# Attention with a two-level mixture of experts: units 30 to 41 of the script reordered, late rows of v loaded at their beginning, item 3 turned on TensorE

## The chip, the cores and the metric

The kernel runs on one core of one Trainium2 chip. The core has five engines that run side by side, each with its own program, in order: TensorE (PE in the profile; its weight loads are PEld), VectorE (DVE), ScalarE (ACT), GpSimd (POOL) and SyncE (SP). They wait for one another by semaphores. SyncE and GpSimd issue DMA transfers here; GpSimd's are indirect, by a list of row numbers. The metric is the device time of one execution in microseconds, as the median of several runs.

## The reference, cut to what matters

Channel attention over four batches: the columns of q and k are normed over the 3648 rows of a batch, a 256 x 256 score matrix is softmaxed, and v is multiplied by it. The result, 14592 rows of 256, goes through a mixture of experts: each row picks one of four groups and one of four experts in it (both by argmax), and each expert is two matrix products with a ReLU between.

```python
qn = q / (np.linalg.norm(q, axis=1, keepdims=True) + 1e-06)
kn = k / (np.linalg.norm(k, axis=1, keepdims=True) + 1e-06)
s = kn.transpose(0, 2, 1) @ qn / tau
...
attn = v @ a                                  # a = softmax(s); (4, 3648, 256)
x = attn.reshape(14592, 256)
g_idx = np.argmax(x @ w_group, axis=1)        # 4 groups
e_idx = np.argmax(xg @ w_expert[g], axis=1)   # 4 experts in each
h = np.maximum(xg[mask_e] @ w1[g, e], 0.0)    # 256 -> 1024
ye = h @ w2[g, e]                             # 1024 -> 256
out[tok_idx] = combined[:, None] * ye         # by the two softmax weights
```

## The kernel before

**Units.** A batch is cut into eight units: seven of 4 x 128 rows and one of 64 rows; four batches make 32 units. Each unit passes two stages. In the first its q and k are loaded and a score matrix is added up on TensorE (tile sacc, L210). After the eighth unit of a batch softmax(b) turns it into the matrix ahi, alo (the two parts of a split that keeps full precision with fast products), through the steps sm, se, ax, atp, awp and ahi. In the second stage a unit's rows of v are loaded (x_load, L278, tile vr), turned by eight TensorE transposes (x_tr, L290, tile vtr), split by ScalarE into vth (L291) and by VectorE into vtl (L292), and multiplied (x_mm, L309, tile xmm: for each of four blocks of 128 rows six matmuls). ScalarE copies each block into xs (L312); VectorE copies its 20 logits into L (L315). Turns of unit u+1 are issued ahead of the products of unit u.

**Routing.** routing(b, j0, j1) is a generator over 16 or 13 blocks of 128 rows, advanced by calls of advance(). It finds each row's expert (m, z, oh: L333 to L355), counts (inc L359, rs L363, two small matmuls pp on TensorE L365, bs L369), and gives each row a slot in a table sorted by expert (sf, si: L376, L378) and a weight (RECIPROCAL into xs, L391). Then GpSimd writes the rows to the table x_sorted, one indirect DMA for 128 rows (scatter, L411, some 1.5 us each on GpSimd with what stands between). After the first half of batch 2 has been routed, tables_pre (L504 to L462 in the lists) finds the first three items.

**Items.** An item is 512 rows of one expert; there are 28. The first three (KPRE) are taken from rows of the batches 0, 1 and the first half of 2 and read by plain DMA (fetch_x, L622); the others are gathered by GpSimd (L485, tile xg) once all rows are in the table. An item's rows are turned into xth, xtl, and each of its eight blocks has six matmuls hmm (ffn1, L827), a ReLU by ScalarE (hh, L831) and VectorE (hl, L832), and twelve matmuls yacc (ffn2, L843) two blocks later. The weights w1, w2 of an item are loaded into raw buffers by SyncE (fetch_w, L609) and split into halves by ScalarE (wh, L654) and VectorE (wl, L655). The first three items are turned by eight TensorE transposes (split_x, L689, tile xtr) with copies by ScalarE (L690) and VectorE (L691). Items from the fourth on (number 3) are turned by sixteen DMAs that re-block them (quads_of, L632, tile xq) and one VectorE STREAM_TRANSPOSE (turn_x, L676, tile xT).

**Order.** Up to unit 29 of the first stage a scheduler orders the engines. Then come script units t = 30 to 41 (TM = 30, k = t - TM = 0 to 11), in which the second stage's unit is x = t - 10 = 20 to 31; from there to the beginning of the items the program order written in the code is each engine's order. After that a scheduler has TensorE, ScalarE and VectorE until item 2, while SyncE and GpSimd stay in written order.

**Space.** v has three buffers (vp). q, k and their squares stand in a pool sp_ that is closed at k = 1. A ring of ten tiles (RING) is shared in turn by the xs of the units, the xg, xq and xT of the items and the results ys: a new tile waits until the one ten places back has been read. So xs of unit 31 takes the place of xs of unit 22, and xg of item 1 that of unit 21. There are three raw buffers for weights.

Of the kernel before, what the change touches and what calls it, by code (L numbers as in the profile page):

```python
# [52 lines left out]
XOFF = GPB + 2  # L53
TM = US - 2
# [3 lines left out]
def attention_moe(ctx: ExitStack, tc, q, k, v, tau, w_group, w_expert, w1, w2, out):  # L58
# [216 lines left out]
    def x_load(u):  # L275
        rows, nj = rows_of(u % GPB)
        vr = vp.tile([P, GJ, C], F32, tag="vr", name="vr", bufs=3)
        SP.dma_start(vr[:rows, :nj, :], tiles_of(v, u // GPB, u % GPB))  # L278
        xu[u] = dict(vr=vr)
# [15 lines left out]
    def x_mm(u, mid=None):  # L295
# [17 lines left out]
        if mid is not None:  # L313
            mid()
# [8 lines left out]
    def routing(b, j0=0, j1=NJ):  # L323
# [68 lines left out]
        pend.extend(((b, j0), now[0], j, si) for j in range(nj))  # L392

# [263 lines left out]
    def split_w(i, which, part=None):  # L657

        if not whs:
            for n in range(4):  # L660
                for l, nm in ((whs, "wh"), (wls, "wl")):
                    l.append(wp.tile([P, 2048], F32R, name=f"{nm}{n}", bufs=1) if n < 3 else None)
# [16 lines left out]
    def split_x(d):  # L679
# [18 lines left out]
        tokens(d["ids"], d["xg"][:, :, C], slot4, d["nv"], None if d is items[0] or "xT" in d else ins)  # L698
# [68 lines left out]
    soft = lambda n=1: [next(sgen, None) for _ in range(n)]  # L767
    for t in range(TM, len(xs_at)):
# [3 lines left out]
        if x + 2 < UX:  # L772
            x_load(x + 2)
        if k == 0:
            soft(2)
        if x + 1 < UX:
            x_tr(x + 1)
        if k == 0:
            s_mm(US - 2)
            s_mm(US - 1)  # L780
            advance(2)
            soft()
        if k == 1:
            sp_.close()
        if k == 2:
            soft(2)
        if k == 4:
            wp = ctx.enter_context(tc.tile_pool(name="wp", bufs=4))
            fetch_w(items[0], tb_pre, 0, "w1")
            fetch_w(items[0], tb_pre, 0, "w2")  # L790
        if x == UX - 3:
            fetch_x(items[0], tb_pre, 0)
        if x == UX - 1:
# [3 lines left out]
        def mid():  # L797
# [15 lines left out]
        if k > 8:  # L813
            advance(1)
        scatter(8)
        queue(x)
    vp_.close()
# [230 lines left out]
    for n in range(len(seq) + lag):  # L1048
        if n == 1:
            fetch_w(items[1], tb_pre, 1, "w1")  # L1050
# [7 lines left out]
        if n < len(seq):  # L1058
# [18 lines left out]
            if f == 7 and KPRE <= i + 2 < NBIG:  # L1077
# [45 lines left out]
        if n >= 1:  # L1123
            advance(20 if n >= 3 else 1)
# [87 lines left out]
```

## Time and profile before

| | us |
|---|---|
| three runs: lowest, median, highest | 1006.2, 1006.58, 1008.39 |
| profiled execution | 1007.67 |
| its span, first to last instruction | 1005.9 |

| engine | busy in the span, us | share |
|---|---|---|
| TensorE | 937.9 | 93% |
| VectorE | 610.2 | 61% |
| ScalarE | 469.7 | 47% |
| GpSimd | 351.9 | 35% |

How to read it: a row of a timeline has its start in us from the beginning of the span, its length, the engine, the line, the operation, the tiles written and read, and in brackets the time for which the engine stood idle just before, with what ended that. A row with "x8" is eight instructions of a kind in a row. "issue" means that the profile shows no other cause. PEclk is the share of TensorE's full clock. The first 30 script units take some 195 us of the span, the twelve in question end near 275 us, and the items fill the rest.

### The profile page before, as it was taken

What the parts mean: (1) busy time and instruction counts of PE and PEld (TensorE: products, weight loads), DVE (VectorE), ACT (ScalarE), POOL (GpSimd) and SP (SyncE); (2) the same over time, 40 slices, a digit from 0 to 9 for tenths busy, and PEclk for the clock granted to TensorE, in tenths of its full rate; (3) what the DMA queues carried; (4) which work ended last, traced back from release to release, by engine and by line L of the source; (5) the groups of instructions that cost most, each with busy time, mean ns of one, the idle gap of its engine ahead of it and who ended that gap; (6) DMA issues with size and microseconds to landing.
All of it is one profiled execution on the core that took longest, in us unless ns stands there. A gap on an engine that the chain in (4) does not pass through costs nothing.

```text
span 1005.9 us, 17880 instructions
## 1 busy us (share of the span) xinstructions
PE 937.9 (93%) x6228; PEld 820.5 (82%) x6228; DVE 610.2 (61%) x1140; ACT 469.7 (47%) x738; POOL 351.9 (35%) x426
## 2 busy tenths in 40 slices
PE   7998999886799569999999999999999999999994
PEld 6898989876688458888888888888888888888884
DVE  6888868655699355555555555555555645555541
ACT  6787567544553034444444444444444444444431
POOL 0005879854668613222222231222222222222111
PEclk9999999987899879999999999999999999999998
DMA  8947688336545345677777777777777677767730
GB/s 299 357 175 262 224 271 266 126 98 223 184 157 214 104 132 166 227 233 233 236 232 233 230 237 226 237 233 242 239 230 236 228 239 236 234 230 239 227 131 26
DMA packets 163188, 215.06 MB, mean 214 GB/s; under 512 B 67635, under 2 KB 121659, under 8 KB 163088
## 3 DMA queue, kind: packets, MB, share of 16 engines
q1 hardware_dynamic: 146512, 168.70, 52.9%
q0 software_dynamic: 15088, 45.10, 12.2%
q8 instruction: 51, 0.84, 0.4%
q14 instruction: 49, 0.40, 0.1%
q10 hardware_dynamic: 1488, 0.02, 0.1%
HBM read 170.33 MB, written 31.39 MB: 201 GB/s over the span
## 4 chain that ended last, share of the span: by engine, by line
PE 61%; issue 2%; SPq 1%; POOL 1%; DMA 0%; DVE 0%; ACT 0%; POOLq 0%; DVEq 0%; ACTq 0%
PE yacc L843 29%; PE hmm L827 27%; PE qacc L945 2%; PE qmm L928 2%; SPq L632 1%; PE qtr L935 1%; POOL out L853 0%; DMA out<-ys,ids 0%; DMA xq<-xg 0%; PE qxt L919 0%; DVE xT L676 0%; DVE hl L832 0%; POOL x_sorted L564 0%; DVE ys L852 0%; ACT wh L654 0%
## 5 line engine op out<-in xcount | busy, mean ns | idle before, releaser
L832 DVE SCALAR_TENSOR_TENSOR hl<-hmm,hh 128x512 fp32r<-128x512 f32 x224 | 153.8, 687 | 253.3 <-ACT hh L831 246.1
L831 ACT ACTIVATE hh<-hmm 128x512 fp32r<-128x512 f32 x224 | 132.6, 596 | 361.2 <-PE hmm L827 296.3
L853 POOL DMA_INDIRECT out<-ys,ids x112 | 127.7, 1140 | 461.5 <-ACT ys L850 434.1
L843 PE MATMUL yacc<-wh,hl 128*128 128x256 f32 x896 | 253.9, 283 | 17.6 <-DVE hl L832 16.5
L843 PE MATMUL yacc<-wh,hh 128*128 128x256 f32 x896 | 257.4, 287 | 4.5 <-DVE ys L852 4.5
L843 PE MATMUL yacc<-wl,hh 128*128 128x256 f32 x896 | 252.9, 282 | 0.0
L843 PEld LDWEIGHTS yacc<-wh,hh 128*128 128x128 f32 x896 | 169.9, 190 | 29.3 <-issue 12.2
L843 PEld LDWEIGHTS yacc<-wh,hl 128*128 128x128 f32 x896 | 170.4, 190 | 18.1 <-DVE hl L832 17.1
L827 PE MATMUL hmm<-xtl,wh 128*128 128x512 f32 x448 | 179.6, 401 | 3.2 <-DVE xtl L691 3.2
L827 PE MATMUL hmm<-xth,wh 128*128 128x512 f32 x448 | 179.6, 401 | 0.5 <-ACT xs L312 0.3
L827 PE MATMUL hmm<-xth,wl 128*128 128x512 f32 x448 | 177.9, 397 | 0.0
L843 PEld LDWEIGHTS yacc<-wl,hh 128*128 128x128 f32 x896 | 170.1, 190 | 7.9
L411 POOL DMA_INDIRECT x_sorted<-xs,si x116 | 142.4, 1228 | 84.9 <-issue 33.3
L655 DVE TENSOR_TENSOR wl<-wraw,wh 128x1024 fp32r<-128x1024 f32 x112 | 137.0, 1223 | 22.4 <-ACT wh L654 15.5
L654 ACT ACTIVATE wh<-wraw 128x1024 fp32r<-128x1024 f32 x112 | 117.8, 1053 | 4.4 <-DMA wraw<-in_moe_w 2.9
L827 PEld LDWEIGHTS hmm<-xth,wl 128*128 128x128 f32 x448 | 85.0, 190 | 20.5
L827 PEld LDWEIGHTS hmm<-xtl,wh 128*128 128x128 f32 x448 | 85.4, 191 | 14.1 <-DVE xtl L691 3.5
L827 PEld LDWEIGHTS hmm<-xth,wh 128*128 128x128 f32 x448 | 85.7, 191 | 12.4 <-ACT xs L312 1.0
L210 PE MATMUL sacc<-qkraw 128*128 128x256 f32 (+1 forms) x352 | 85.7, 389 | 6.5 <-DMA qkraw<-in_k 6.5
L210 PEld LDWEIGHTS sacc<-qkraw 128*128 128x128 f32 (+1 forms) x352 | 65.6, 195 | 15.4 <-DMA qkraw<-in_q 6.0
L309 PE MATMUL xmm<-ahi,vth 128*128 128x276 f32 (+1 forms) x232 | 71.6, 310 | 3.2 <-ACT xs L312 3.2
L309 PE MATMUL xmm<-alo,vth 128*128 128x276 f32 (+1 forms) x232 | 69.8, 301 | 0.0
(240 smaller groups left out, 1174.0 us busy)
## 6 DMA issues: line engine op xcount, KB each, us to landing
wraw<-in_moe_w SPq DMA_DIRECT2D x56, 1024.0 KB
wraw<-in_moe_w SPq DMA_DIRECT2D x96, 512.0 KB
vr<-in_v SPq DMA_DIRECT2D x28, 512.0 KB
qkraw<-in_q SPq DMA_DIRECT2D x27, 512.0 KB
qkraw<-in_k SPq DMA_DIRECT2D x27, 512.0 KB
xq<-xg SPq DMA_DIRECT2D x400, 32.0 KB
x_sorted<-xs,si POOLq DMA_INDIRECT x116
out<-ys,ids POOLq DMA_INDIRECT x112
```

The lines of the kernel that those rows point to most:

```text
L210: PE.matmul(d["acc"][:, c, :], kt[:rows, 1, cs], qt[:rows, 0, :], start=d.pop("first", True) and c == 0, stop=(g == NG), skip_group_check= ...
L309: PE.matmul(mm[:rows, :NE], vt[:, c, j * P:j * P + rows], at[:, c, :], start=(n == 0), stop=(n == 5))
L411: ins = POOL.indirect_dma_start(out=xs_d, out_offset=bass.IndirectOffsetOnAxis(ap=si[:rows, j:j + 1], axis=0), in_=xs[:rows, t, 0:RW].bitc ...
L654: ACT.activation(whs[n][:, s], raw[:, s], AF.Copy)
L655: DVE.tensor_tensor(wls[n][:, s], raw[:, s], whs[n][:, s], ALU.subtract)
L827: PE.matmul(mm, wt[:, c, fs], xt[:, c, :], start=(n == 0), stop=(n == 5))
L831: ACT.activation(hh, mm, AF.Relu)
L832: d["hl"] = DVE.scalar_tensor_tensor(hl, mm, 0.0, hh, ALU.max, ALU.subtract)
L843: PE.matmul(a, ht[:, tsl], wt[:, f, :], start=(f == 0 and t % 2 == 0 and n == 0), stop=(f == 7 and n == 2), skip_group_check=True)
L853: ins = POOL.indirect_dma_start(out=out, out_offset=bass.IndirectOffsetOnAxis(ap=d["ids"][:, t:t + 1], axis=0), in_=ys[:, t, :], in_offset ...
L928: PE.matmul(mm[r, :], qs["xT"][q % 2][:, c, r], qs["w", p][:, c * 512:(c + 1) * 512], start=(c == 0), stop=(c == 1), tile_position=(0, p * ...
L945: PE.matmul(qs["a"][r, 0:C], qs["hT"][k][:, o:o + PC], qs["w", p][:, f * C:(f + 1) * C], start=(k == 0 and f == 0), stop=(k == 1 and f == ...
```

## The change

x_load gets a second pool. At k = 1 the pool of q and k is closed, and five buffers for v (VX = 5, pool vx) are made in that space; units 24 to 28 are loaded there and 29 to 31 into vp, at k = 1, 2 and 3. Item 0's weights are asked for at k = 5 and 6, its rows at k = 8; vx is closed then, and the split halves of item 0's w2 and of item 1's w1 get a pool of their own (wb). x_mm takes a hook after any of its four blocks instead of one at the end, and the calls of advance() stand at other places (early_, late_); routing has one more step at its end. The split of item 0's w2 leaves the script: its first half follows the last unit, its second half the item's first block. Item 3 loses quads_of and turn_x, so that split_x turns it as it turns the items before.

```diff
-    def x_load(u):
+    def x_load(u, pool=None):
-        vr = vp.tile([P, GJ, C], F32, tag="vr", name="vr", bufs=3)
+        vr = (pool or vp).tile([P, GJ, C], F32, tag="vr", name="vr", bufs=VX if pool else 3)
...
         pend.extend(((b, j0), now[0], j, si) for j in range(nj))
+        yield
...
-        if x + 2 < UX:
+        if k == 0:
             x_load(x + 2)
-        if k == 0:
             soft(2)
+        if k == 1:
+            sp_.close()
+            wp = ctx.enter_context(tc.tile_pool(name="wp", bufs=4))
+            vx = vx_.enter_context(tc.tile_pool(name="vx", bufs=VX))
+            x_load(x + 2)
+            for u in range(x + 3, x + 6):
+                x_load(u, vx)
+        if k == 2:
+            for u in range(x + 5, x + 7):
+                x_load(u, vx)
+        if k == 3:
+            for u in range(UX - 3, UX):
+                x_load(u)
...
-        if k == 4:
-            wp = ctx.enter_context(tc.tile_pool(name="wp", bufs=4))
+        if k == 5:
             fetch_w(items[0], tb_pre, 0, "w1")
+        if k == 6:
             fetch_w(items[0], tb_pre, 0, "w2")
-        if x == UX - 3:
+        if k == 8:
             fetch_x(items[0], tb_pre, 0)
+            vx_.close()
+            wb = ctx.enter_context(tc.tile_pool(name="wb", bufs=4))
...
-        def mid():
+        def early_():
             if k == 0:
                 advance(1)
                 soft()
-            elif k < 7:
-                advance((1, 1, 2, 2, 2, 2)[k - 1])
-
-        x_mm(x, mid)
+            if k == 6:
+                advance(2)
+
+        def late_():
+            if k == 0:
+                advance(2)
+            else:
+                advance({1: 2, 2: 1, 4: 2, 5: 2, 6: 1, 7: 1, 10: 2, 11: 1}.get(k, 0))
+
+        x_mm(x, {1: early_, 3: late_})
...
-        if k in (7, 8):
-            split_w(0, "w1", k - 7)
-        if k in (9, 10):
-            split_w(0, "w2", k - 9)
-        if k > 8:
-            advance(1)
+        if k in (8, 9):
+            split_w(0, "w1", k - 8)
         scatter(8)
         queue(x)
+    split_w(0, "w2", 0)
...
         if n == 1:
+            split_w(0, "w2", 1)
...
-            if f == 7 and KPRE <= i + 2 < NBIG:
+            if f == 7 and KPRE < i + 2 < NBIG:
                 quads_of(items[i + 2])
...
-                if f == 3:
+                if f == 3 and i + 1 > KPRE:
                     turn_x(items[i + 1])
...
-            advance(20 if n >= 3 else 1)
+            advance(20 if n >= 3 else 2)
```

Three places show what this does to the engines' programs. Lines of the changed kernel are a few higher than those of before.

SyncE, round the last loads of v: in before, from the load of item 0's w1 (128x2x1024) and, after the reading of the table tb_pre, w2 (128x8x256) to the last two rows of v, units 30 and 31:

```order
L609 DMA wraw<-in_moe_w 128x2x1024
L606 TENSOR_LOAD tb_pre
L606 ISA x2
L609 ISA
L609 DMA wraw<-in_moe_w 128x8x256
L278 DMA vr<-in_v 128x1024 x3
L621 TENSOR_LOAD tb_pre
L621 ISA x2
L278 DMA vr<-in_v 128x1024
L278 DMA vr<-in_v 64x256
```

The five vr behind the weights are those of units 27 to 31; units 24 to 26 stand ahead of this piece.

In the changed kernel, where the first row is units 24 to 30 and the second unit 31:

```order
L279 DMA vr<-in_v 128x1024 x7
L279 DMA vr<-in_v 64x256
L609 TENSOR_LOAD tb_pre
L609 ISA x2
L612 ISA
L612 DMA wraw<-in_moe_w 128x2x1024
L609 TENSOR_LOAD tb_pre
L609 ISA x2
L612 ISA
L612 DMA wraw<-in_moe_w 128x8x256
```

All loads of v now stand ahead of the table and of item 0's weights.

VectorE, from the copy of the last unit's logits (64x20) on; in before (m, z, oh, sw belong to the second half of batch 3, inc and rs to its first half, hl to item 0, wl_3032 to item 1's w1; wl is the low half of a weight):

```order
L315 COPY L<-xs 64x20
L359 SCALAR_TENSOR_TENSOR inc<-scm_104,oh 128x256
L333 TENSOR_REDUCE m_3457<-L 128x65
L832 SCALAR_TENSOR_TENSOR hl<-hmm,hh 128x512
L336 TENSOR_TENSOR z<-L,m_3457 128x260
L655 TENSOR_TENSOR wl_3032<-wraw,wh_3031 128x1024
L344 SCALAR_TENSOR_TENSOR oh_3463<-z,key_93 128x260
L381 TENSOR_REDUCE sw<-ez 128x65
L345 TENSOR_REDUCE m_3457<-oh_3463 128x65
L832 SCALAR_TENSOR_TENSOR hl<-hmm,hh 128x512
L363 CAST rs<-inc 128x16
```

The count of batch 3's first half follows the logits at once. In the changed kernel (wl_3102 is item 0's w2):

```order
L317 COPY L<-xs 64x20
L658 TENSOR_TENSOR wl_3102<-wraw,wh_3101 128x1024
L335 TENSOR_REDUCE m_3498<-L 128x65
L850 SCALAR_TENSOR_TENSOR hl<-hmm,hh 128x512
L338 TENSOR_TENSOR z<-L,m_3498 128x260
L658 TENSOR_TENSOR wl_3102<-wraw,wh_3101 128x1024
L346 SCALAR_TENSOR_TENSOR oh_3504<-z,key_93 128x260
L383 TENSOR_REDUCE sw<-ez 128x65
L347 TENSOR_REDUCE m_3498<-oh_3504 128x65
L850 SCALAR_TENSOR_TENSOR hl<-hmm,hh 128x512
L361 SCALAR_TENSOR_TENSOR inc<-scm_104,oh 128x256
L348 TENSOR_TENSOR oh_3504<-oh_3504,m_3498 128x260
```

Both halves of item 0's w2 now stand here, ahead of the count (inc) of batch 3's first half; the halves of item 1's w1 come later.

TensorE, in item 2, with tile numbers; in before (hl_4256 is VectorE's part of the block two before hmm_4326; hl_4334, which VectorE makes behind item 3's STREAM_TRANSPOSE, is read two blocks of matmuls further on):

```order
L827 MATMUL hmm_4326<-xtl_4020,wh0_3027 128x512
L827 MATMUL hmm_4326<-xth_4019,wl0_3028 128x512
L843 MATMUL yacc_4261<-wh1_3029,hh_4255 128x256
L843 MATMUL yacc_4261<-wl1_3030,hh_4255 128x256
L843 MATMUL yacc_4261<-wh1_3029,hl_4256 128x256
```

Nothing stands between the block's hmm and the yacc. In the changed kernel at the same block (hmm_4314 is the same step as hmm_4326, hl_4246 as hl_4256):

```order
L845 MATMUL hmm_4314<-xtl_4027,wh0_3099 128x512
L845 MATMUL hmm_4314<-xth_4026,wl0_3100 128x512
L692 MATMUL xtr_4327<-ident_73,xg_4022 128x128 x4
L692 MATMUL xtr_4334<-ident_73,xg_4022 128x128 x4
L861 MATMUL yacc_4251<-wh1_3101,hh_4245 128x256
L861 MATMUL yacc_4251<-wl1_3102,hh_4245 128x256
L861 MATMUL yacc_4251<-wh1_3101,hl_4246 128x256
```

Item 3's eight transposes stand ahead of that block's yacc and read xg as it was gathered.

More of the change, by code (lines that the diff above doesn't have):

```diff
@@ L53 @@
 XOFF = GPB + 2
+VX = 5
 TM = US - 2
@@ L293, in x_tr, with x_mm @@
         x["th"], x["tl"] = th, tl
-    def x_mm(u, mid=None):
+    def x_mm(u, hooks=None):
+        hooks = hooks or {}
         b, g = divmod(u, GPB)
@@ L312, in x_mm @@
             ACT.activation(xs[:rows, j, :], mm[:rows, :NE], AF.Copy)
-        if mid is not None:
-            mid()
+            if j in hooks:
+                hooks[j]()
         DVE.tensor_copy(d["L"][:rows, g * GJ:g * GJ + nj, :], xs[:rows, :nj, C:NE])
@@ L661, in split_w @@
                 for l, nm in ((whs, "wh"), (wls, "wl")):
-                    l.append(wp.tile([P, 2048], F32R, name=f"{nm}{n}", bufs=1) if n < 3 else None)
+                    l.append((wp if n == 0 else wb).tile([P, 2048], F32R, name=f"{nm}{n}", bufs=1) if n < 3 else None)
         if i == 1 and which == "w2":
@@ L697, in split_x @@
             DVE.tensor_copy(d["wc"], d["xg"][:, :, C + 1])
-        tokens(d["ids"], d["xg"][:, :, C], slot4, d["nv"], None if d is items[0] or "xT" in d else ins)
+        tokens(d["ids"], d["xg"][:, :, C], slot4, d["nv"], None if d is items[0] or "xT" in d or d is items[KPRE] else ins)
     items = [dict() for _ in range(NBIG)]
@@ L767, in attention_moe @@
     soft = lambda n=1: [next(sgen, None) for _ in range(n)]
+    vx_ = ctx.enter_context(ExitStack())
     for t in range(TM, len(xs_at)):
@@ L780, in attention_moe @@
             s_mm(US - 1)
[L781 to L784, printed above, removed]
+            advance(1)
         if k == 2:
             soft(2)
-        if k == 4:
-            wp = ctx.enter_context(tc.tile_pool(name="wp", bufs=4))
+        if k == 5:
             fetch_w(items[0], tb_pre, 0, "w1")
+        if k == 6:
             fetch_w(items[0], tb_pre, 0, "w2")
-        if x == UX - 3:
+        if k == 8:
             fetch_x(items[0], tb_pre, 0)
+            vx_.close()
+            wb = ctx.enter_context(tc.tile_pool(name="wb", bufs=4))
         if x == UX - 1:
@@ L800, in mid @@
                 soft()
-            elif k < 7:
-                advance((1, 1, 2, 2, 2, 2)[k - 1])
-        x_mm(x, mid)
+            if k == 6:
[6 more added lines that the diff above has]
+        x_mm(x, {1: early_, 3: late_})
         if k == 0:
-            advance(1)
+            soft()
         if k == 1:
             soft(3)
-        if k in (7, 8):
-            split_w(0, "w1", k - 7)
-        if k in (9, 10):
-            split_w(0, "w2", k - 9)
-        if k > 8:
-            advance(1)
+        if k in (8, 9):
+            split_w(0, "w1", k - 8)
         scatter(8)
         queue(x)
+    split_w(0, "w2", 0)
     vp_.close()
```

## The prediction

> **What bounds the kernel now.** I read a table of windows first (busy time of each engine in each stretch), then the timeline round TensorE's own waits, then what released them.
>
> ```profile
> core 0: us, PE busy (x) PEld busy (x) DVE busy (x) ACT busy (x) POOL busy (x), PEclk, DMA share, GB/s
> 235.00:241.00 6.00, 0.96 (x5) 0.99 (x6) 0.00 (x0) 0.00 (x0) 0.05 (x1) 0.50 0.95 378
> 275.00:335.00 60.00, 53.53 (x329) 47.68 (x330) 57.81 (x192) 24.44 (x39) 43.32 (x66) 0.96 0.47 165
> 345.00:361.00 16.00, 0.60 (x4) 0.35 (x3) 1.82 (x2) 0.74 (x1) 3.84 (x4) 0.68 0.51 142
> 375.00:975.00 600.00, 598.95 (x4090) 510.58 (x4089) 333.66 (x481) 259.42 (x389) 147.57 (x132) 1.00 0.72 228
> ```
>
> From 375 us on TensorE is busy 598.95 of 600 us at full clock: nothing else sets the time there, so whatever lets that stretch begin earlier comes off the end one for one. Ahead of it lie two holes, 235 to 241 and 345 to 361, and between 275 and 335 VectorE is the full engine (57.81 of 60). The change edits the work on both sides of the holes. TensorE's own idle times there, from its timeline (the bracket is the idle time before the row and what ended it):
>
> ```profile
> 200.79 0.20 PE L365 MATMUL pp<-rs,tri 128*128 128x16 bf16 x1 [2.10 <-DVE rs L363]
> ...
> 213.92 0.27 PE L290 MATMUL vtr<-ident,vr 64*128 64x64 f32 x1 [3.98 <-DVE vtl L292]
> ...
> 233.15 0.17 PE L365 MATMUL pp<-rs,tri 128*128 128x16 bf16 x1 [1.18 <-DVE L L315]
> ...
> 240.04 1.94 PE L290 MATMUL vtr<-ident,vr 128*128 128x128 f32 x8 [6.70 <-DMA vr<-in_v]
> ...
> 242.01 0.43 PE L309 MATMUL xmm<-alo,vth 128*128 128x276 f32 x1
> 242.24 0.43 PE L309 MATMUL xmm<-ahi,vtl 128*128 128x276 f32 x1
> ...
> 360.85 0.58 PE L843 MATMUL yacc<-wh,hl 128*128 128x256 f32 x1 [15.40 <-DVE hl L832]
> 361.23 0.41 PE L843 MATMUL yacc<-wh,hh 128*128 128x256 f32 x1
> 361.44 0.41 PE L843 MATMUL yacc<-wl,hh 128*128 128x256 f32 x1
> ```
>
> **Part 1, the early loads of v.** The queue of SyncE in before runs in order:
>
> ```profile
> 227.21 1.81 SPq L609 DMA_DIRECT2D wraw<-in_moe_w  x2
> 229.12 18.68 SPq L278 DMA_DIRECT2D vr<-in_v  x5
> ```
>
> The five last loads of v stand behind the weights of item 0, which wait for a table until 227.21, and TensorE finds its row missing: 6.70 us. After the change the loads of units 24 to 29 are issued once the last score matmul is done, at about 198.7. The window 235 to 241 moved 378 GB/s; six loads of 0.52 MB at that rate take 8.3 us, so they are there by about 209. Unit 24's turns stand behind those of unit 23 (213.92 in before, at most 6 us sooner in after) and unit 22's matmuls (some 3 us), so they come at 211 at the earliest. The 6.70 goes, and nothing on that queue replaces it: item 0's weights come behind the loads, and their table is still the later of the two.
>
> The re-spaced routing calls take two more waits away. The count matmuls pp stand behind twelve matmuls of unit 20, so the 2.10 is filled; unit 22's vtl stands ahead of the table's first rows on VectorE, so most of the 3.98 goes. These idle times, with 0.33 behind the 3.98 and the 1.18, sum to 14.3 us. With each long one goes the slow clock behind it: xmm matmuls there follow at 0.23 us instead of the usual 0.13 (242.01 to 242.24 above), about 13, 19 and 13 of them, so some 4.5 us. I keep 3 us: the eight turns of a unit still wait for VectorE's vtl of the unit before, and pp now stands in the middle of unit 26 and waits there for VectorE. Unit 26's matmuls, at 241.63 before, then begin 16 us earlier, at about 225.5.
>
> That is not yet the gain, since the units end in a queue of GpSimd:
>
> ```profile
> 244.56 0.53 DVE L376 TENSOR_REDUCE sf<-inc 128x13 f32<-128x208 f32 x1
> ...
> 246.63 0.84 DVE L391 RECIPROCAL xs<-se 128x4 f32<-128x4 f32 x4
> ```
>
> ```profile
> 247.59 1.00 POOL L411 DMA_INDIRECT x_sorted<-xs,si  x1 [12.54 <-issue]
> ...
> 252.02 1.79 POOL L411 DMA_INDIRECT x_sorted<-xs,si  x1 [0.16 <-issue]
> ...
> 265.38 2.00 POOL L411 DMA_INDIRECT x_sorted<-xs,si  x1 [0.17 <-issue]
> ...
> 267.87 0.97 POOL L411 DMA_INDIRECT x_sorted<-xs,si  x1 [0.17 <-issue]
> ```
>
> ```profile
> 274.64 0.39 ACT L312 ACTIVATE xs<-xmm 64x276 f32<-64x276 f32 x1 [8.40 <-DMA x_sorted<-xs,si]
> ```
>
> ScalarE's copy of the last unit, xs of unit 31 at T = 274.64, waits until unit 22's rows have left its ring slot: the last of their scatters is issued from 267.87 to 268.84 and lands 5.8 us later. All of item 0's blocks stand behind that copy on ScalarE, so the items begin with the scatters and not with the units. The scatters follow the reciprocals of batch 2's second half, which end at 247.47, 5.8 us after unit 26's first matmul. In after they stand behind unit 26's last copy and the vtl of unit 28: at 225.5 + 9.8 = 235.3, **12.2 us earlier**. (Unit 26 takes 4.7 us with the wait at pp, its copy and the vtl 2, the stages from sf to the reciprocals 2.9, as at 244.56 to 247.47 in before.) If scatters and landing take what they took, T' = 262.4. Four of these scatters took 1.79 to 2.00 us instead of 0.98, the first and last of them shown, 3.6 us in all, and the landing lag can be shorter:
>
> ```profile
> 263.87 0.35 SPq L622 DMA_DIRECT2D xg<-x_sorted  x1
> ```
>
> This load waits for unit 21's last scatter, issued by 261.72, so that one landed within 2.15 us; the 5.8 fell together with item 1's weights. With all of that gone T' = 255.1. I take 259.0, near the middle, since the same weights follow the same scatters in after: **15.6 us earlier**, ends 12.2 and 19.5. The Trainium skill, page "DMA: Bandwidth & Descriptors", section "Anatomy of one DMA — SWDGE (gpsimd) path", gives a scatter's way as some 2.0 us plus its bytes at 436 GB/s; for 0.14 MB that would be an estimated 2.3 us, and by it the sum would be some 1.7 us lower than with my middle. The 5.8 of the row at 274.64 speaks against it and the 2.15 of the row at 263.87 for it. A new wait of TensorE stands here: unit 30's matmuls will be done near 246, so TensorE will stand some 5 to 9 us ahead of T'.
>
> **Part 2, item 3 without the 16 turns by DMA.**
>
> ```profile
> 342.19 0.70 POOL xg L485
> ...
> 346.61 0.76 SPq L632
> ...
> 356.49 1.88 DMA xq<-xg
> 358.98 1.25 DVE xT L676
> 360.22 0.59 DVE hl L832
> 360.85 2.50 PE yacc L843 x10
> ```
>
> This piece of the chain of waits is the second hole: gather of item 3 issued at 342.19, landed when the first of sixteen issues begins at 346.61, the issues, their landing, one transpose on VectorE, and hl, which TensorE wants and which stands behind that transpose. From landing to restart 14.2 us, and all of it goes. But the eight TensorE transposes do not stand where the hole was. They stand ahead of the yacc of hl_4246, whose like in before (hl_4256) begins two blocks sooner than the hole, at 339.42:
>
> ```profile
> 339.42 0.28 PE L843 MATMUL yacc<-wh,hh 128*128 128x256 f32 x1
> ...
> 345.17 0.28 PE L843 MATMUL yacc<-wl,hh 128*128 128x256 f32 x1
> ```
>
> Between 339.42 and 345.45, where the hole begins, lie 6.0 us of matmuls that before did ahead of the hole and after does behind it. All of TensorE now waits at its xtr for the gather's landing. The transposes cost
>
> ```profile
> 278.54 1.00 PE L689 MATMUL xtr<-ident,xg 128*128 128x128 f32 x7
> ```
>
> some 1.0 us warm, and their copies lie beside four blocks of matmuls. They will not be warm: after the hole at 240.04 eight vtr took 1.94, and the yacc at 361.23 and 361.44 step by 0.21 where warm ones step by 0.12. I count 2.0 us of slow clock in after, and 1.5 in before, paid behind 360.85.
>
> When does the gather land? In before 72.0 us after T (346.61 less 274.64). The two splits of item 0's second matrix are moved from beside the units to behind T; the first of them on VectorE in before:
>
> ```profile
> 259.64 1.23 DVE L655 TENSOR_TENSOR wl<-wraw,wh 128x1024 fp32r<-128x1024 f32 x1 [0.67 <-ACT wh L654]
> ```
>
> There VectorE's idle time covered them; behind T VectorE is full, and they stand ahead of si of batch 3's first half, on which all of GpSimd's work up to the gather hangs. Two of 1.23 are 2.5; one idle gap there is filled, so 2.3: landing at T' + 74.3, with 72 and 76 as ends (the splits hidden; the splits at full price and their ScalarE halves waited for). TensorE comes to xtr at T' + 67 (339.42 less 274.64, and the 2.3) and **stands some 7 us**. What before did at 360.85, T + 86.2, after does at T' + 74.3 + 1.0 + 2.0 + 6.0 = T' + 83.3. With the 1.5 of slow clock that before pays behind that point the gain is **4.4 us**, ends 2.7 and 6.7.
>
> Item 4 still goes by DMA. In before its 16 issues followed at
>
> ```profile
> 358.64 12.15 SPq L632 DMA_DIRECT2D xq<-xg  x16
> ```
>
> behind item 3's, and VectorE read them without a wait:
>
> ```profile
> 378.23 1.23 DVE L676 STREAM_TRANSPOSE xT<-xq 128x1024 f32<-128x1024 f32 x1
> ```
>
> In after only its own gather holds them:
>
> ```profile
> 348.71 1.05 POOL L485 DMA_INDIRECT xg<-x_sorted,ix_big  x1 [0.31 <-issue]
> ```
>
> That is 6.5 us behind item 3's; with 12.15 of issues and 1.9 of landing 20.6 us after item 3's landing, while VectorE reaches the transpose some 26 us after it (9.0 to the old restart's place and 17.4 from there, 378.23 less 360.85). Nothing is paid.
>
> **Sum.** From the profiled execution, 1007.67 us (span 1005.9 and 1.8 around it): 1007.67 - 15.6 - 4.4 = 987.7. That execution lies 1.1 us above the median of 1006.58, so about **986.6**, and **987** as the forecast.
>
> **The rivals.**
> (a) *The scatters hold T harder.* If the stages of batch 2's routing queue longer behind vtl and copies on VectorE than I count, T moves by the 6.7 of the loads alone to 10 us, and the turn gives its 2.7: 994 to 997. For it: the 12.54 us for which GpSimd stands idle ahead of 247.59 end with VectorE's reciprocals. Against: the stages ahead of them are called a unit or more apart, and stand ahead of nothing that TensorE needs soon.
> (b) *More than I count.* T' at 255, splits hidden: 19.5 + 6.7, so 980. For it: VectorE's share of 57.81 in 60 leaves 2.2 us, and the 2.15 above.
> (c) *TensorE never stands at xtr.* If batch 3's routing, called two steps at a time, gives si as early as before, and TensorE is itself late through VectorE, the stand shrinks from 7 us to less than 3; this gives the 6.7 of the ends at most, and 984. It is inside the forecast.
> (d) *The loads do not do what they say.* If they cannot start at 198.7, since q and k's space is freed late, 6.70 stays and T moves by some 5: 998.
> (e) *Slower.* TensorE, in order, stands at xtr for the gather, behind all scatters of batch 3 and the first writes of item 0 on GpSimd. Each us by which that is late costs one. It ends later than before once the landing comes after 360.85 + 1.5 - 9.0 = 353.3, which is 20.0 us beyond my 259.0 + 74.3. That needs T' not to move at all (15.6) and the splits to delay batch 3's routing by 6.7 instead of 2.3, as they would if each stage lost its place behind hl: 1007 to 1012.
>
> **How the numbers follow.** Forecast 0.68 (981 to 992, from the ends 12.2 + 2.7 and 19.5 + 6.7, and (c) in it); (a) 0.14; (b) 0.08; (d) 0.05; (e) 0.03; within 0.2% of before, which is about what a measurement of this kernel can tell from no change, 0.02. The range 979 to 995 holds the forecast, most of (b) and the nearer part of (a). Faster 0.95, same 0.02, slower 0.03.
>
> **What would show it.** Right: no vr wait on TensorE; reciprocals of batch 2's second half near 235; xs of unit 31 near 259, released by a scatter, with TensorE idle ahead of it; no xq before item 4; a stand of 5 to 9 us ahead of item 3's xtr, ended by its gather near 333; TensorE full from there. Wrong: xs of unit 31 beyond 263; the gather's landing more than 77 us behind it; a wait at item 4's transpose; a stand ahead of item 0 that weights end.

## The result, and the profile after

| | before | after |
|---|---|---|
| median, us (range, runs) | 1007.34 (1006.2 to 1008.39, 4) | 992.1 (988.23 to 992.58, 4) |
| profiled execution, us | 1007.67 | 991.87 |
| its span, us | 1005.9 | 990.1 |

The ratio is 0.9841, with a 95% interval of 0.9813 to 0.9869: 15.2 us faster. The forecast was 987, the range 979 to 995.

The table of windows of the changed kernel, cut at its own holes (columns as in the table of before; two windows are left out):

```profile
core 0: us, PE busy (x) PEld busy (x) DVE busy (x) ACT busy (x) POOL busy (x), PEclk, DMA share, GB/s
235.00:260.00 25.00, 18.75 (x119) 16.17 (x117) 13.08 (x39) 10.50 (x24) 18.86 (x29) 0.86 0.47 158
...
275.00:320.00 45.00, 39.03 (x250) 35.00 (x248) 44.20 (x146) 16.74 (x26) 39.70 (x61) 0.98 0.51 178
320.00:335.00 15.00, 6.70 (x30) 5.62 (x30) 4.61 (x13) 1.20 (x2) 9.16 (x10) 0.73 0.49 159
335.00:350.00 15.00, 14.44 (x89) 13.39 (x90) 6.52 (x11) 5.48 (x8) 3.00 (x3) 0.89 0.30 88
350.00:960.00 610.00, 606.66 (x4132) 516.37 (x4131) 336.81 (x486) 262.93 (x394) 150.10 (x134) 1.00 0.70 226
```

The hole of 235 to 241 is gone, and that of 345 to 361 has become a shorter one between 320 and 335 (8.3 us without TensorE in that window). VectorE is still the full engine ahead of it (44.20 of 45). TensorE fills the rest less closely than before: 606.66 of 610, where it was 598.95 of 600.

TensorE's own timeline of the changed kernel:

```profile
198.08 0.18 PE L367 MATMUL pp<-rs,tri 128*128 128x16 bf16 x1 [0.55 <-DVE rs L365]
...
222.68 1.03 PE L291 MATMUL vtr<-ident,vr 128*128 128x128 f32 x8
223.47 0.37 PE L311 MATMUL xmm<-ahi,vth 128*128 128x276 f32 x1
...
227.87 0.17 PE L367 MATMUL pp<-rs,tri 128*128 128x16 bf16 x1 [2.64 <-DVE inc L361]
...
229.92 1.91 PE L291 MATMUL vtr<-ident,vr 128*128 128x128 f32 x8
...
335.56 1.95 PE L692 MATMUL xtr<-ident,xg 128*128 128x128 f32 x8 [7.62 <-DMA xg<-x_sorted,ix_big]
```

The wait of 2.10 at the first pp is 0.55, and no row of this stretch waits for a load of v. The row at 223.47 is the first matmul of unit 26. In that unit stands a new wait, 2.64 us at pp, and the eight turns behind it take 1.91 us instead of the 1.03 of the turns ahead of it (222.68): the clock has fallen, to a granted 0.50 between 230 and 232 us. At 335.56 TensorE stands 7.62 us for item 3's gather.

The steps between, from the timelines of VectorE, ScalarE, GpSimd and SyncE of the changed kernel:

```profile
235.17 0.84 DVE L393 RECIPROCAL xs<-se 128x4 f32<-128x4 f32 x4
```

```profile
260.86 0.39 ACT L314 ACTIVATE xs<-xmm 64x276 f32<-64x276 f32 x1 [11.96 <-DMA x_sorted<-xs,si]
```

```profile
254.39 0.97 POOL L414 DMA_INDIRECT x_sorted<-xs,si  x1 [0.17 <-issue]
...
273.26 0.99 POOL L414 DMA_INDIRECT x_sorted<-xs,si  x1 [15.96 <-DVE oh L357]
...
331.26 1.06 POOL L488 DMA_INDIRECT xg<-x_sorted,ix_big  x1 [2.18 <-issue]
```

```profile
195.83 11.46 SPq L279 DMA_DIRECT2D vr<-in_v  x8
```

All eight loads of v are issued by 207.3. The reciprocals of batch 2's second half end at 236.01 (247.47 before), unit 31's copy into xs comes at T' = 260.86 (T = 274.64 before), and item 3's gather is issued at 331.26 (342.19 before).

**Where the 15.7 us of the two profiles came from.** Five marks cut an execution into pieces whose sum is its length: a, the start of the last group of score matmuls (the last work that is the same in both kernels); T; g, the issue of item 3's gather; q, the first matmul of the small pieces that are worked off between the items (tile qxt); e, the last one of them (tile qacc). Two of the marks, from TensorE's timelines, of before:

```profile
197.56 1.13 PE L210 MATMUL sacc<-qkraw 64*128 64x256 f32 x4
...
392.39 0.41 PE L919 MATMUL qxt<-ident,qxg 128*128 128x128 f32 x2
...
972.56 1.93 PE L945 MATMUL qacc<-wraw,qhT 128*32 128x256 f32 x32
```

and of the changed kernel:

```profile
194.68 1.13 PE L211 MATMUL sacc<-qkraw 64*128 64x256 f32 x4
...
373.50 0.41 PE L937 MATMUL qxt<-ident,qxg 128*128 128x128 f32 x2
...
956.88 1.93 PE L963 MATMUL qacc<-wraw,qhT 128*32 128x256 f32 x32
```

The mark a lies 2.9 us earlier, in work that the change does not touch: a difference of the two executions. From a to g 144.6 became 136.6, 8.0 less. From g to q 50.2 became 42.2, 8.0 less. From q to e 580.2 became 583.4, 3.2 more, where both kernels run the same code. The sum is -15.7. The first of these pieces is chance, and the last is taken up in the closing section. So a single pair of profiles misleads by some us, and the experiments below are read by the same marks over all their profiles.

### The profile page after: what moved, and what is told of

The parts are those of the page before. It is cut to its first block, busy times and chain, and to the rows that moved or that the text cites. A ratio compares the mean times of both kernels' runs of the same rounds, so it can differ in the third digit from the quotient of the medians.

```text
span 990.1 us, 17864 instructions
## 1 busy us (share of the span) xinstructions
PE 934.6 (94%) x6236; PEld 815.8 (82%) x6236; DVE 609.7 (62%) x1140; ACT 470.6 (48%) x739; POOL 345.4 (35%) x426
## 3 DMA queue, kind: packets, MB, share of 16 engines
q0 software_dynamic: 15088, 45.10, 12.4%
## 4 chain that ended last, share of the span: by engine, by line
PE 63%; issue 2%; POOL 0%; DMA 0%; DVE 0%; ACT 0%; POOLq 0%; DVEq 0%; ACTq 0%
PE yacc L861 29%; PE hmm L845 28%; PE qacc L963 2%; PE qmm L946 2%; PE qtr L953 1%; DMA xg<-x_sorted,ix_big 0%; POOL out L871 0%; PE xtr L692 0%; PE qxt L937 0%; POOL x_sorted L567 0%; DVE ys L870 0%; ACT wh L657 0%; ACT hh L849 0%; DVE hl L850 0%; POOLq L1110 0%
## 5 line engine op out<-in xcount | busy, mean ns | idle before, releaser
L861 PEld LDWEIGHTS yacc<-wh,hh 128*128 128x128 f32 x896 | 170.0, 190 | 28.7 <-issue 13.3
L414 POOL DMA_INDIRECT x_sorted<-xs,si x116 | 136.5, 1177 | 81.1 <-issue 32.9
L845 PEld LDWEIGHTS hmm<-xtl,wh 128*128 128x128 f32 x448 | 85.4, 191 | 13.3 <-DVE xtl L694 2.5
L311 PE MATMUL xmm<-ahi,vth 128*128 128x276 f32 (+1 forms) x232 | 69.9, 303 | 3.1 <-ACT xs L314 2.9
L311 PE MATMUL xmm<-alo,vth 128*128 128x276 f32 (+1 forms) x232 | 67.8, 293 | 0.0
```

The costliest lines, as they stand in the source:

```text
L311: PE.matmul(mm[:rows, :NE], vt[:, c, j * P:j * P + rows], at[:, c, :], start=(n == 0), stop=(n == 5))
L414: ins = POOL.indirect_dma_start(out=xs_d, out_offset=bass.IndirectOffsetOnAxis(ap=si[:rows, j:j + 1], axis=0), in_=xs[:rows, t, 0:RW].bitc ...
L845: PE.matmul(mm, wt[:, c, fs], xt[:, c, :], start=(n == 0), stop=(n == 5))
L861: PE.matmul(a, ht[:, tsl], wt[:, f, :], start=(f == 0 and t % 2 == 0 and n == 0), stop=(f == 7 and n == 2), skip_group_check=True)
```

## The experiments

Two theories stood at the beginning. Mine: script and turn each give their own piece, and they add. The rival: the two share one piece, because item 3's gather is what TensorE waits for in either case, so that one of them alone gives nearly all. Ratios are to the kernel before, run beside each.

**The changed kernel again.**

> The changed kernel once more. If the 3.2 us that its profiled execution lost between 375 and 975 us come from stops of TensorE that belong to this kernel's order, they stand again at the same matmuls and the time is 992 within 1. If they belong to the execution (one of four earlier ones took 988.2 against 991.9 to 992.6), the stops fall at other places or are fewer, and the time lies anywhere from 988 to 993.

993.41 us (992.08 to 996.52), ratio 0.9868, 0.9833 to 0.9903. T' came at 262.11, 67.1 behind a (66.2 in the first profile), and the stand at xtr was 6.43 us. The time is 0.4 us above the upper end of both expectations (993), and from q to e it takes 583.8 again. The result holds.

**The turn alone.** Before, with item 3 turned on TensorE:

```diff
-        tokens(d["ids"], d["xg"][:, :, C], slot4, d["nv"], None if d is items[0] or "xT" in d else ins)
+        tokens(d["ids"], d["xg"][:, :, C], slot4, d["nv"], None if d is items[0] or "xT" in d or d is items[KPRE] else ins)
...
-            if f == 7 and KPRE <= i + 2 < NBIG:
+            if f == 7 and KPRE < i + 2 < NBIG:
                 quads_of(items[i + 2])
...
-                if f == 3:
+                if f == 3 and i + 1 > KPRE:
                     turn_x(items[i + 1])
```

The edit of tokens(), which belongs to the whole change too, only keeps item 3 free of an ordering on VectorE that the items turned by DMA do not have either.

> The kernel before, with item 3 alone turned on TensorE. Theory: the script is as before, so xs of unit 31 stays at 274.6 and the gather of item 3 lands at 346.6; TensorE stands ahead of item 3's transposes until then (7 us) and 9.0 us of work follow to the place where it restarted at 360.85 with 1.5 us of slow clock to come, so 6.7 us less than before, about 1000. Rival 1: the whole chain of sixteen issues, landing and transpose comes off, 14.2 us, about 993. Rival 2: the wait only changes its name, 1006.

998.24 us (997.36 to 999.41), ratio 0.9911, 0.9881 to 0.9941: some 8 us, near the 6.7 expected and far from both rivals' 993 and 1006. TensorE's timeline of this kernel:

```profile
234.79 1.94 PE L290 MATMUL vtr<-ident,vr 128*128 128x128 f32 x8 [6.49 <-DMA vr<-in_v]
...
345.10 1.96 PE L689 MATMUL xtr<-ident,xg 128*128 128x128 f32 x8 [6.69 <-DMA xg<-x_sorted,ix_big]
```

The wait for v is there as before, and the hole of 15.40 us has become the stand of 6.69 ahead of cold transposes. From g to q it takes 43.0 us.

**The script alone.** After, with item 3's sixteen DMAs put back (the same edits the other way round):

> The changed kernel, with item 3 turned by sixteen DMAs and VectorE as before. Theory: xs of unit 31 at 260.9 and the gather's landing at 335.6 as in the changed kernel, then 14.2 us to TensorE's restart, at 349.8 against 360.85: 11 us less than before, about 996, 4 above the changed kernel. Rival: the reordered script brings all of the 15 us, 992. Rival: without the new turn the script's gain is hidden behind the DMA chain, 1003 or more.

998.55 us (995.55 to 1001.91), ratio 0.9906, 0.9872 to 0.9939: some 8 us, less than the 11 expected. On TensorE's timeline the old hole is back:

```profile
351.46 0.58 PE L861 MATMUL yacc<-wh,hl 128*128 128x256 f32 x1 [14.90 <-DVE hl L850]
```

8.0 of the turn and 7.7 of the script against 13 to 15 of both: within the some 3 us by which these ratios are uncertain, they add. The rival falls, since neither alone gives nearly all.

**The loads alone.** Before, with the eight loads of v at the script's beginning and all routing calls and splits where they were:

```diff
...
+        if k == 1:
+            sp_.close()
+            wp = ctx.enter_context(tc.tile_pool(name="wp", bufs=4))
+            vx = vx_.enter_context(tc.tile_pool(name="vx", bufs=VX))
+            x_load(x + 2)
+            for u in range(x + 3, x + 6):
+                x_load(u, vx)
+        if k == 2:
+            for u in range(x + 5, x + 7):
+                x_load(u, vx)
+        if k == 3:
+            for u in range(UX - 3, UX):
+                x_load(u)
...
```

> The kernel before, with the early loads of v alone: routing called where it was, w2 split in the script, item 3 by DMA. Theory: TensorE's 6.5 to 6.7 us wait for v goes and with it the slow clock behind it (1.3), the waits of 2 and 4 us for VectorE stay; the second half of batch 2 is routed some 7 us earlier, xs of unit 31 follows by as much, and the time is about 999. Rival: the scatters of batch 2's first half or VectorE hold the units instead, and less than 3 us remain: 1004.

998.76 us (996.63 to 1000.4), ratio 0.9908, 0.9878 to 0.9938. Its waits on TensorE, and the first matmul of unit 26:

```profile
198.11 0.18 PE L367 MATMUL pp<-rs,tri 128*128 128x16 bf16 x1 [1.95 <-DVE rs L365]
...
211.34 0.37 PE L291 MATMUL vtr<-ident,vr 64*128 64x64 f32 x1 [3.93 <-DVE vtl L293]
...
231.21 0.17 PE L367 MATMUL pp<-rs,tri 128*128 128x16 bf16 x1 [0.34 <-DVE rs L365]
...
232.14 0.38 PE L311 MATMUL xmm<-ahi,vth 128*128 128x276 f32 x1
```

The two waits that the re-spaced calls were to take away stand here in full, and yet the time is that of the whole script alone (998.55). In exchange the pp that waits 2.64 us inside unit 26 in the changed kernel stands ahead of that unit here and waits 0.34. On TensorE the re-spacing does win: unit 26 begins 37.1 us behind the mark a here (a is 195.03) and 28.8 in the changed kernel. But the reciprocals come 43.1 behind a, against 41.1 to 44.0 in the new script's profiles in the table below: routing on VectorE takes next to nothing of it. The whole script differs from this kernel in a second edit, the splits of w2 behind T. T comes 70.9 behind a here and 66.2 to 69.1 there, but from T to g it takes 67.1 here and 70.0 to 70.4 there, so that g comes 138.0 behind a in both (in the mean there). In the time, the loads carry the script's gain; what the re-spaced calls give by themselves, this one profile does not show.

**The loads late again.** After, with the last five loads of v behind item 0's weights:

```diff
+        if k == 5:
+            fetch_w(items[0], tb_pre, 0, "w1")
+            fetch_w(items[0], tb_pre, 0, "w2")
+        if x + 2 < UX:
+            x_load(x + 2)
...
```

The eight early loads and the two calls of fetch_w at k = 5 and 6 are taken out for it.

> The changed kernel, with the last five loads of v behind item 0's weights as before. Theory: TensorE waits some 6 us for unit 27's rows again, near 223 to 229, the reciprocals of batch 2's second half come 4 to 5 us later than in the changed kernel (240.5 in place of 236), xs of unit 31 as well, and the time is some 4.5 above the changed kernel's 992 to 993, about 997. Rival: the loads are hidden behind the wait for VectorE at pp (2.6 us) and the ring slot, and the time stays within 1 us of the changed kernel.

1003.0 us (996.95 to 1005.75, 10 runs), ratio 0.9955, 0.993 to 0.9981: some 10 us slower than the changed kernel, and 6 slower than expected. On its TensorE timeline:

```profile
234.28 1.94 PE L291 MATMUL vtr<-ident,vr 128*128 128x128 f32 x8 [8.91 <-DMA vr<-in_v]
```

The wait is back at 8.91 us, longer than the 6.70 of before, and from a to g this execution takes 145.7, as before. The reciprocals come 49.5 behind a (196.25), as late as in the old script (49.4 in the mean) and not 4 to 5 us behind the changed kernel as expected. With the turn's gain in it, the re-spaced script without its loads is worth nothing or less: this kernel is slower than the turn alone (998.24), and it pays for the splits behind T (T to g 70.2).

**The splits of w2 back into the script.**

```diff
+        if k in (9, 10):
+            split_w(0, "w2", k - 9)
         scatter(8)
...
-    split_w(0, "w2", 0)
...
-            split_w(0, "w2", 1)
```

> The changed kernel, with the split of item 0's second matrix put back into the script (half each behind units 29 and 30). Theory: xs of unit 31 is held by the scatters and stays at 260.9; VectorE has 2.5 us less to do behind it, so batch 3's first scatter comes 2.4 us earlier (271 in place of 273.3), so does item 3's gather, and the time is 2.4 us below the changed kernel, about 989.5. Rival: the splits beside the units delay the units' copies and turns, xs of unit 31 comes later by as much, and the time is 992 or more.

990.44 us (988.57 to 992.85), ratio 0.9843, 0.981 to 0.9876. On GpSimd's timeline the first scatter of batch 3, in the second row below, comes 9.65 us behind this kernel's T' of 260.13; in the changed kernel it came 12.40 behind:

```profile
255.69 0.93 POOL L414 DMA_INDIRECT x_sorted<-xs,si  x1 [0.28 <-POOL xs L413]
269.78 0.99 POOL L414 DMA_INDIRECT x_sorted<-xs,si  x1 [12.83 <-DVE oh L357]
```

So the splits cost 2.75 us of the chain there. Of the whole 1.7 to 3.0 us are gained against the two sets of runs of the changed kernel, and the intervals overlap.

**Unit 31's rows in a tile of their own.** The ring slot no longer holds the copy:

```diff
-        xs = ring(GJ, NE, name="xs")
+        xs = ring(GJ, NE, name="xs") if u < UX - 1 else rp.tile([P, 1, NE], F32, name="xs_own", bufs=1)
```

> The changed kernel, with the last unit's copy (xs of unit 31) in a tile of its own, outside the ring of ten. Theory: that copy no longer waits for unit 22's scatters, it comes when its matmuls are done, near 251; then item 0's first block on ScalarE waits for item 1's weights, which land near 257, 4 us before its time in the changed kernel; all that follows comes 4 us earlier, 988.5. Rival: the scatters themselves hold the items (batch 3's first scatter and with it the gather move by less than 1 us), 992.

989.29 us (988.18 to 990.21), ratio 0.9816, 0.9793 to 0.9839. ScalarE's timeline of this kernel shows what it waits for in the slot's place:

```profile
246.83 0.39 ACT L314 ACTIVATE xs_own<-xmm 64x276 f32<-64x276 f32 x1
247.13 1.04 ACT L657 ACTIVATE wh<-wraw 128x1024 fp32r<-128x1024 f32 x1
260.40 1.06 ACT L657 ACTIVATE wh<-wraw 128x1024 fp32r<-128x1024 f32 x1 [12.22 <-DMA wraw<-in_moe_w]
```

The copy begins 14 us sooner, at 246.83. After item 0's first split of w2 (247.13) ScalarE's next work is the first split of item 1's weights, and it stands 12.22 us for these. They were issued late:

```profile
250.19 0.31 SPq L625 DMA_DIRECT2D xg<-x_sorted  x1
251.73 1.67 SPq L612 DMA_DIRECT2D wraw<-in_moe_w  x2
```

They stand on SyncE behind the rows of item 1 (250.19), which wait for the ring slot of unit 21 in its turn. So a second wait on the scatters ends at 260.40, only 0.5 us ahead of the 260.86 at which the first ended in the changed kernel. Still the tile gave something: the time is 2.8 and 4.1 us below the two sets of runs of the changed kernel, near the 988.5 expected, and g comes 133.9 us behind a, where it came 136.6 and 137.3. VectorE does its half of that first split of w2 inside the wait here (250.86) and behind it in the changed kernel (262.23).

**Item 3's transposes two blocks later.**

```diff
-                if f == 4:
+                if f == (6 if i + 1 == KPRE else 4):
                     split_x(items[i + 1])
```

> The changed kernel, with item 3's transposes two blocks of matmuls later (behind block 6 in place of block 4). Theory: TensorE does 5.65 us of matmuls while it waited for the gather; it stands some 2 us instead of 7.6 and the time falls by 5 to 5.7, to about 987. Rival: the copies of the transposed rows by ScalarE and VectorE come too late for item 3's first matmuls, and the wait only moves there: within 1.5 us of the changed kernel.

985.37 us (982.67 to 991.92), ratio 0.9792, 0.9738 to 0.9846. TensorE's timeline:

```profile
337.97 1.19 PE L692 MATMUL xtr<-ident,xg 128*128 128x128 f32 x8 [1.15 <-DMA xg<-x_sorted,ix_big]
```

The stand falls from 7.62 to 1.15 us and the transposes are fast, 1.19 instead of 1.95. From g to q it takes 35.6 us, 6.7 less than in the changed kernel. The two blocks that my prediction counted as moved behind the wait were a real loss, and this gets them back.

**Combined.** Late transposes with the splits back, and both with the tile of its own:

> Transposes of item 3 at f = 6 and the w2 splits back inside the script. If each edit takes its own piece off the path, the gains add: 985.4 of the late transposes alone, less the 3.0 that the splits gave alone, 982.5. If the late transposes already hide the landing of item 3's gather (1.15 us of stand were left in that run), the 3 us by which the gather lands sooner save at most those 1.15: 984.2, and the stand ahead of item 3's transposes falls to nothing.

> The same two edits, and the weights of unit 31's tokens in a tile of their own. Sum of the three gains measured alone: 992.1 less 6.7, 1.7 and 2.8, 980.9. If only the stand of 1.15 was left to win once the transposes are late, 984.2 as in the run beside it, with the softmax of unit 31 some 2 us sooner and no gain from that.

985.68 us (981.7 to 986.67, 6 runs), ratio 0.9787, 0.9762 to 0.9813; and 982.41 (978.56 to 986.97, 6 runs), ratio 0.9766, 0.9737 to 0.9795. The splits add nothing to the late transposes. Their timelines show why, the first kernel's row and then the second's:

```profile
335.98 1.95 PE L692 MATMUL xtr<-ident,xg 128*128 128x128 f32 x8 [4.47 <-DMA xg<-x_sorted,ix_big]
```

```profile
334.87 1.95 PE L692 MATMUL xtr<-ident,xg 128*128 128x128 f32 x8 [4.31 <-DMA xg<-x_sorted,ix_big]
```

Without the splits behind T, TensorE reaches xtr sooner too, 69.9 us behind T in the first of these kernels (335.98 less 4.47, and T at 261.58) against 73.4 with late transposes alone, while the gather has landed 74.4 behind T against 74.6. So the stand grows from 1.15 to 4.47 us: I had expected it to vanish. Why the gather did not land sooner was not tried; its issue took 1.86 us on GpSimd there and 1.06 with late transposes alone. The version with all three is the fastest measured; whether the tile of its own gives it the last 3 us is not settled by these runs, whose ranges overlap.

**Two more profiles with the old script,** on another chip, to see what of the first profile was chance:

> The kernel before once more, for a second profile. In the first one the copy of unit 31 came 77.1 us behind the last group of score matmuls; with the same script and only item 3's turn changed it came 72.4 us behind it. If the slow scatters and their landing in the first profile were a chance of one execution, this profile shows about 72 (70 to 74) and an idle time below 4 us at that copy; then the script's gain is some 6 us. If they belong to the kernel before, it shows 76 to 78 with some 8 us of idle time, and the script's gain is 10 to 11.

> The kernel before with item 3 turned on TensorE, once more, for a second profile. The same script as in the kernel before: 72 us from the last group of score matmuls to the copy of unit 31 if its first profile is typical, 77 if that of the kernel before is.

Before took 1000.19 us there and 1000.0 in a second run, and the turn alone 996.73, in one run. The turn's gain is only some 3.4 us in these, since this execution with the turn takes some 4 us longer from a to g (the table below). ScalarE's copy of unit 31, of before on that chip:

```profile
268.90 0.40 ACT L312 ACTIVATE xs<-xmm 64x276 f32<-64x276 f32 x1 [6.03 <-PE hmm L827]
```

73.6 us behind a (195.28), as the one expectation had it, though with 6.03 us of idle time and not below 4; the kernel with the turn showed 77.9, near the other. (The row names a matmul of item 0 as what ended the wait. The copy comes 6.1 us behind the end of unit 22's last scatter, 5.4 to 6.4 in the other profiles of the table, so I take its landing to have ended it.) So the old script takes 72.4 to 77.9 us from a to T by chance of the execution. One value decides nothing; the four must be taken together:

| kernel, profile | a | a to reciprocals' end | a to T | a to g | g to q | q to e |
|---|---|---|---|---|---|---|
| before | 197.56 | 49.9 | 77.1 | 144.6 | 50.2 | 580.2 |
| before, other chip | 195.28 | 48.4 | 73.6 | 141.1 | 49.9 | 578.4 |
| turn alone | 194.03 | 48.2 | 72.4 | 146.8 | 43.0 | 581.0 |
| turn alone, other chip | 194.74 | 51.0 | 77.9 | 145.4 | 42.8 | 578.4 |
| after | 194.68 | 41.3 | 66.2 | 136.6 | 42.2 | 583.4 |
| after again | 195.04 | 41.1 | 67.1 | 137.3 | 43.0 | 583.8 |
| script alone | 194.11 | 44.0 | 68.8 | 138.8 | 50.5 | 582.8 |
| late transposes | 194.29 | 43.8 | 69.1 | 139.3 | 35.6 | 582.8 |

The first four have the old script, the last four the new one. Their means: to the reciprocals 49.4 and 42.6, to T 75.2 and 67.8, to g 144.5 and 138.0. **The script gives 6.5 us at g.** From g to q the three by DMA take 50.2 and the four that turn on TensorE at the old place 42.8 (means). **The turn gives 7.5 us.** Together 14.0 up to q, against 15.2 and 12.9 between the medians; from q to e the last four take 3.7 us longer than the first four in the mean, so the agreement is a rough one.

Two things hardly move. T to g takes 67.5 us in three of the old script's profiles and 70.0 to 70.4 in the new one's; the 2.7 between them are the splits that now stand behind T. Only the first profile of the turn alone breaks this, with 74.4: there T came early, at 72.4, ScalarE then waited 3.18 us for a matmul of item 0 (270.95), and so T was not what the items waited for. Without that profile the script's gain at g is 5.7. The four profiles of the new script that stand outside the table (splits back, tile of its own, and the two combined versions) have their reciprocals 39.8 to 41.6 behind a; with them the mean of the new script is 41.6 instead of 42.6.

## Why the prediction was right, and where it was not

The direction was right, and so were the two pieces, the wait for v and the hole at item 3. The time lay in the range, 5 us above the forecast and at the upper end of the forecast's own 981 to 992. That it did so is in part luck: T', the largest term of the sum, came 7.5 us earlier, outside its own ends of 12.2 and 19.5, and the range held the time because it reached into rival (a) and because the turn gave more than said. By the steps:

- **The wait for v goes** (6.70): right. No such wait is left, and the late loads brought 8.91 back. The loads were done in time.
- **The waits of 2.10 and 3.98 go with the re-spaced calls**: right on TensorE. Unit 26 began at 223.47, 28.8 us behind a where the forecast had 27.9 (225.5 less 197.56), with the 3 us kept for new waits. But the step from there to the time failed: with the loads alone unit 26 began 8.3 us later and the reciprocals came about as soon (43.1).
- **Reciprocals 9.8 us behind unit 26's first matmul**: mis-sized. It was 12.5 (236.01 less 223.47). My parts, 4.7, 2 and 2.9, made 9.6 and not 9.8, and the first two were too small. I allowed the unit 4.7 us with its wait at pp; it took 6.4 up to the turns at 229.92, 2.64 of them that wait, and slow matmuls behind it, and the vtl of unit 28 ended 3.2 later instead of 2. The absolute 235.3 against 236.01 looks close only because this execution had started its script 2.9 us earlier.
- **Half of the scatters' delay goes too** (3.4 us): wrong. From the reciprocals' end to T the old script takes 25.9 us in the mean of its four profiles, the new one 25.2. The last scatter of unit 22 ends at 255.36 and the copy follows at 260.86, 5.5 us later, against 5.8 before, and it is 5.4 to 6.4 in all eight profiles of the table: the short landing of 2.15 on which I had leaned does not come at this place. The sentence on the Trainium skill, page "DMA: Bandwidth & Descriptors", section "Anatomy of one DMA — SWDGE (gpsimd) path" (some 2.0 us plus bytes, an estimate of 2.3 us here) finds no support in these rows, and the measured 5.4 to 6.4 decide.
- **T' 15.6 us earlier**: this is the term that failed. It measured 7.5 us by the means (13.8 in the pair of profiles, 2.9 of which lie ahead of the change). Of the missing 8.1, 5.4 are the reciprocals (6.8 us earlier by the means instead of 12.2; 7.8 with the four profiles outside the table) and 2.7 the scatters (0.7 instead of 3.4). Rival (a) had named the mechanism of the first, routing that queues longer behind vtl and copies, and its 6.7 to 10 us for T hold the measurement; its price for the turn (2.7) does not.
- **A new wait of 5 to 9 us ahead of T'**: TensorE stands 7.5 us between unit 31's matmuls and T', but in three waits, 2.17 us for VectorE's xtl (251.12), 2.52 for the rows of item 1 (254.60) and 2.82 for ScalarE behind its copy (261.30). Only the last hangs on T'.
- **The splits cost 2.3**: right. The first scatter of batch 3 follows T by 10.0 us in before (284.60) and 12.4 in after, and putting the splits back took off 2.75. The landing came at T' + 74.7, forecast T' + 74.3.
- **The turn**: right, somewhat more than said. Its row of the sum, 4.4, was 6.7 less those 2.3; the 6.7 measured 7.5. The stand was 7.62 (7 forecast), the transposes cold at 1.95 as said, and the 6.0 us of matmuls moved behind the wait came back when the transposes were put later, with the stand 6.5 us shorter. Item 4's transpose on VectorE shows no wait, as said:

```profile
359.34 1.23 DVE L679 STREAM_TRANSPOSE xT<-xq 128x1024 f32<-128x1024 f32 x1
```

- **TensorE full from there**: right to 99%, but not without a loss; the 3.2 us between q and e are in the last section.
- **Sum**: 20.0 forecast, of it 13.3 at g and 6.7 behind; 6.5 and 7.5 measured over the profiles.

Rivals (c) and (d) did not come: TensorE stood 7.62 us at xtr, and the loads began at 195.83. (b) and (e) needed a T' of 255 and one that did not move.

## What to carry to other kernels

Ask of a wait that is removed what stands behind it, on the same engine and on the next, and how far: here a new wait of 2.64 us with its slow clock, routing on VectorE that took up little of the time won on TensorE, and scatters that kept their delay, left half of what the sum had promised for the script, and where the ring slot was taken out of the way, a second wait ended only half a us ahead of it. An operation that waits for a transfer belongs, in an in-order engine, as late as its reader allows: eight transposes moved two blocks gave about as much as the whole reordered script. And before a single timeline is used as the base of a sum, measure in a second profile how far its marks move by themselves (here 5 us at T).

## What the runs showed of the hardware that was not expected

**Short stops of TensorE where weights are loaded.** In the changed kernel, TensorE's timeline behind q has stops of 0.2 to 0.7 us that no semaphore explains; here with SyncE's row of the same window:

```profile
460.13 3.09 SPq L927 DMA_DIRECT2D wraw<-in_moe_w  x3
...
460.17 0.48 PE L845 MATMUL hmm<-xth,wl 128*128 128x512 f32 x1 [0.34 <-issue]
...
461.60 0.40 PE L845 MATMUL hmm<-xtl,wh 128*128 128x512 f32 x1 [0.71 <-issue]
```

All seven of this profile, 3.1 us in sum, lie within 3 us of a load of weights that SyncE issues; most such loads bring no stop. The windows from 400 to 960 us, of the changed kernel and then of before on the other chip:

```profile
400.00:960.00 560.00, 556.81 (x3812) 473.04 (x3811) 307.30 (x442) 240.95 (x361) 137.66 (x123) 1.00 0.71 228
```

```profile
400.00:960.00 560.00, 560.00 (x3824) 478.29 (x3823) 317.94 (x448) 244.66 (x365) 134.58 (x119) 1.00 0.73 234
```

On the other chip TensorE is busy 560.00 of 560, with no stop at all, and q to e takes 578.4 us in both kernels run there; elsewhere it takes 580.2 to 583.8 in the table. The stops are not all chance: three of them stand at the same distance from q in both profiles of the changed kernel, 364.1, 391.0 and 491.7 us, and others stand at one place in one of them only. All four profiles of the new script in the table take longer from q to e (582.8 to 583.8) than the four of the old one (578.4 to 581.0). What the stops are, and whether the changed kernel itself brings more of them, was not tried and stays open: it was not run on the chip that shows none.

**The clock falls after some short waits, and the length of the wait does not say which.** In the changed kernel the turns behind the wait of 2.64 us took 1.91, those behind 7.62 took 1.95; with the late transposes, behind 1.15, they took 1.19. In before the matmuls behind 2.10 were slow (step 0.23), too. But in the changed kernel those behind 2.17 (251.12) stayed fast, 0.24 a step between two hmm (251.46 to 251.70) where 0.23 is usual, and with the late loads waits of 0.95 and 0.33 us (206.24, 207.69) were followed by steps of 0.23 between xmm. Nor does the fall come at once: behind the 2.64 the steps are 0.13 us up to 228.90, and slow from 229.02 to some 232.3. The Trainium skill, page "TensorE: Matmul & The Clock Gate", section "Part 1: The HAM clock gate", puts the fall after an idle window of some 3.4 us. The rows show slow matmuls after less than that; the measurement decides for this kernel, and what counted as idle ahead of each fall no run here shows.

**The start of the script moves.** The mark a, with the same code ahead of it, lies between 194.03 and 197.56 us in these profiles.
